# Sooner swaps, a denser opening and a last layer on 128 rows in a convolution and SwiGLU kernel

## The chip, the cores and the metric

The kernel runs on one core of one Trainium2 chip. The metric is the device time of one execution in microseconds (us). Of the kernel before, three timed executions and one profiled execution are shown.

## What is computed

An input `x` of 8 sequences of 4096 tokens with 192 channels goes through a causal depthwise filter of 7 taps (each of 8 heads has its own softmaxed taps for its 24 channels), and the result through a SwiGLU block with 1536 hidden columns.

```python
w = softmax(weight)                       # 8 heads x 7 taps
x_unf = x_pad[:, idx, :]                  # windows of 7 tokens, zeros ahead of the sequence
out = einsum('hk,bskhg->bshg', w, x_unf)  # 24 channels for each head
g, val = x @ w_gate, x @ w_val            # 192 -> 1536, on 32768 tokens
return (silu(g) * val) @ w_out            # 1536 -> 192
```

## The kernel before

**Blocks, chunks, pairs.** The 32768 tokens are 64 blocks of 512. Each block has 12 chunks, one for each 128 hidden columns. Two blocks are a pair, and the filter is made pair by pair: 32 pairs of 24 chunks. The 192 channels are 128 (A) and 64 (B or C).

**First layer.** `Block.first` makes a chunk's gate and value: three steps, and in each step one product on rows 0 to 63 of the array (gate, L428) and one on rows 64 to 127 (value, L429). The two run side by side. Because both halves of the channels must pass through both halves of the array, each filtered tile `xc` has a copy `xs` with its halves swapped. `swapped` (L339) makes it with two transfers from SyncE's queue (L341, L342). `Block.gate` then applies silu on ScalarE (L433) and multiplies with the value on VectorE into `h` (L435). Gates have two banks of PSUM, values three, in rotation.

**Second layer.** `Block.piece` (L440) multiplies 64 rows of `h` with 64 rows of `w_out`. Its two halves run side by side into two banks of `acc`, in two passes: after the first pass the two banks change their halves. Between the passes stands a mark: an empty instruction in SyncE's queue that waits for the last product of the first pass, and for which the first product of the second pass waits (L335). A half of a block (256 tokens) takes 24 units, four at each chunk. A block's units run one block behind its first layer, apart from the first four, which stand at its own last chunk (`lead=4`). Marks therefore come at chunks 1 and 7, and at chunks 4 and 10 a half is complete: ScalarE copies it (L478), SyncE stores it (L470).

**The filter.** Three groups make a pair: g=0 (A of the first block), g=1 (B of both), g=2 (A of the second). Each is transposed on VectorE, its taps are shared out among ScalarE (L365, L358), VectorE (L375) and GpSimd (L380, L387), and GpSimd's last sum writes `xc` (L393). VectorE's running sum starts in a bank of PSUM of its own (`run`). `plan_group` puts each step behind a chunk by `PLAN`. For g=0, 1 and 2, `start` is -16, -24 and -8, and `swap` is counted from there: the swaps stand behind chunks -5, -11 and +7 of the pair, and `load` puts the next pair's loads of x behind chunks 1, 2 and 8 of a block. `opening` has the same steps for pair 1, its last number being the swap.

**Order.** Every engine works off its instructions in the order written. SyncE's queue holds loads, swaps, marks and stores in one order, so that what waits in it holds all that follows.

**Opening and end.** Pair 0 has a filter of its own. Products of zeros into `idle` (`warm`) precede it; `turn_a` transposes x, `spread(0)` multiplies the softmaxed taps out to 128 rows, VectorE makes diagonals (L284) of them, and `conv_a` (L304) filters on TensorE. Its results D0, D1 and D2 are copied by ScalarE (L495 to L499). Behind the last block, `run` makes the rest of its second layer in four banks, in two passes with marks between them, and two stores of 256 tokens follow (L631 to L647).

Of the kernel before, what the change touches and what calls it, by code (L numbers as in the profile page):

```python
# [12 lines left out]
PLAN = dict(  # L13
    start=(-16, -24, -8), turn=-2,
    acts=((3, 5), (2, 4), (2, 4)), dves=(1, 3), pool=4, join=5, npool=(2, 2, 3),
    swap=(11, 13, 15),
    load=((2, -47), (3, -40), (0, -34), (1, -28)),
    opening=(
# [3 lines left out]
    ),  # L22
    gate=2, val=3, lead=4,
)


# [1 line left out]
def kernel(  # L28
# [9 lines left out]
    nc = tc.nc  # L38
    fp32 = mybir.dt.float32
# [9 lines left out]
    P = 128  # L49
    DB = D - P  # L50
    grp = D // H
    SUBS = 4
    TB = P * SUBS
    NCH = Dff // P
# [4 lines left out]
    n_pairs = NT // (2 * TB)  # L59
# [22 lines left out]
    def emit_load(q, part):  # L82
        head = q % ppb == 0
        if part == 2:
            squares[q, "A"] = headA if head else xpool.tile(
                [P, HIST + 2 * TB], fp32, tag="sqA", name="sqA"
            )
            squares[q, "B"] = headB if head else xpool.tile(
                [P, HIST + TB], fp32, tag="sqB", name="sqB"
            )  # L90
        for k in range(2):
            quad = 2 * (part % 2) + k
            if part < 2:
                tile_, t0, n, c = squares[q, "A"], 0, 2 * TB, SQ * quad
            else:
                tile_, t0, n, c = squares[q, "B"], TB * (part % 2), TB, P + SQ * k
            skip = HIST if head and t0 == 0 else 0
            row = q * 2 * TB + t0 - HIST + skip
            n = n // SQ + 1 - skip // SQ
            nc.sync.dma_start(  # L100
                out=tile_[quad * SQ : (quad + 1) * SQ, skip:].rearrange("p (n c) -> p n c", c=SQ),
                in_=x_flat[row : row + n * SQ, c : c + SQ].rearrange("(n p) c -> p n c", p=SQ),
            )
# [19 lines left out]
    for lo, hi in ((0, 2), (2, SUBS), (SUBS, 2 * SUBS)):  # L123
        nc.sync.dma_start(
            out=x_sb[:, lo:hi, :],
            in_=x_flat[lo * P : hi * P, :].rearrange("(s p) d -> p s d", p=P),
# [5 lines left out]
    wo_r = wpool.tile([P, NCH, D], fp16, tag="wo_sb", name="wo_sb")  # L132
# [5 lines left out]
    def load_w(lo, hi, which):  # L138
# [15 lines left out]
        out=mask, in_=mask, pattern=[[1, D]],  # L154
# [3 lines left out]
        out=mask, in_=mask, pattern=[[-1, D]],  # L158
# [33 lines left out]
    for b in range(2):  # L192
# [22 lines left out]
    early = {  # L215
        n: pool0.tile(shape, dt, tag=n, name=n)
        for n, shape, dt in (
            ("xtA", [P, TB], fp32),
            ("xtC", [P, DB + TB], fp16),
            ("sum0", [P, TB], fp32),  # L220
            ("sum1", [P, TB], fp32),
            ("idle", [P, TB], fp32),
            ("sum2", [P, TB], fp32),
# [5 lines left out]
    def warm(*repeats):  # L229
        for r in repeats:  # L230
            nc.tensor.matmul(  # L231
                early["idle"][:, 0 : r * P].rearrange("p (r c) -> p r c", c=P), zeros,
                zeros.unsqueeze(1).to_broadcast([P, r, P]), start=True, stop=True,
            )
# [11 lines left out]
    def turn_a(subs):  # L246
        for s in subs:
            ins = nc.tensor.matmul(  # L248
                early["xtA"][:, ts(s, P)], x16[:, s, colA], ident, start=True, stop=True
            )  # L250
        return ins
# [3 lines left out]
    def spread(g):  # L255
        nc.tensor.matmul(  # L256
            early[f"taps{g}"], (mask[:, 0:P], own)[g], raw, start=True, stop=True
        )

    warm(*6 * (SUBS,))  # L260
    turned = turn_a((0, 1))

    if n_pairs > 1:
        sync_after(nc.sync.nop(), turned, "squares after x")
        for part, _ in PLAN["load"]:
            emit_load(1, part)
    spread(0)
    turn_a((2, 3))
    warm(SUBS, 2)

    xcA, xcC, xcC1, xcA1 = (
        const_pool.tile([P, pad + TB], fp16, tag=n, name=n) for n in ("xcA", "xcC", "xcC1", "xcA1")
# [6 lines left out]
    hi = const_pool.tile([P, 2, K], fp16, tag="hi", name="hi")  # L279
    lo = const_pool.tile([P, K], fp16, tag="lo", name="lo")  # L280
# [20 lines left out]
    def conv_a(d, first):  # L301
        for k in range(K):
            for r, bank in ((slice(0, DB), "sum0"), (slice(DB, P), "sum1")):
                nc.tensor.matmul(  # L304
                    early[bank], d[r, k, :], xcA[r, k : k + TB],
                    start=first and k == 0, stop=not first and k == K - 1,
                )
# [37 lines left out]
    class Group:  # L345
# [24 lines left out]
        def dve_tap(self, k, last):  # L370
            v, s = self.tap(k)
            run = self.aD
            if last:
                self.aD = cpool.tile([P, TB], fp32, tag="aD", name="aD")
            nc.vector.scalar_tensor_tensor(  # L375
                out=self.aD, in0=v, scalar=s, in1=run, op0=ALU.mult, op1=ALU.add
            )
# [21 lines left out]
    class Block:  # L399
# [19 lines left out]

        def first(self, j, steps=range(3)):  # L420
            if 0 in steps:
                self.g[j] = gpool.tile([P, TB], fp32, tag="gate", name="gate")
                self.v[j] = vpool.tile([P, TB], fp32, tag="val", name="val")
            g, v, f = self.g[j], self.v[j], ts(j, P)
            lo, hi = self.operands()
            for i in steps:
                (a, ca), (b, cb) = lo[i], hi[i]
                nc.tensor.matmul(g, w[0:DB, ca, f], a[0:DB, :], start=(i == 0), stop=(i == 2))  # L428
                nc.tensor.matmul(v, w[DB:P, cb, f], b[DB:P, :], start=(i == 0), stop=(i == 2))  # L429
# [52 lines left out]
    D0, D1, D2, D2b = (  # L482
        const_pool.tile([P, TB], fp16, tag=n, name=n) for n in ("D0", "D1", "D2", "D2b")
    )
# [5 lines left out]
    def tapA1(k, xt=None):  # L490
        return (xt or early["xtA1"][:, DB - pad :])[:, k : k + TB], wn[:, 0, k : k + 1]
# [3 lines left out]
    nc.scalar.copy(D0, early["sum0"])  # L495
    nc.scalar.copy(D1, early["sum1"])
    nc.scalar.copy(xcC1, early["xtC1"][:, DB - pad :])
    nc.scalar.mul(actA1[1], *tapA1(5, xcA1))
    nc.scalar.copy(D2, early["sum2"])  # L499
    v, s = tapA1(0)  # L500
    nc.vector.tensor_scalar(sumA1, v, scalar1=s, scalar2=None, op0=ALU.mult)
    for k in range(1, 4):
        v, s = tapA1(k)
        nc.vector.scalar_tensor_tensor(
            out=sumA1, in0=v, scalar=s, in1=sumA1, op0=ALU.mult, op1=ALU.add
# [3 lines left out]
    v, s = tapA1(6, xcA1)  # L509
# [11 lines left out]
    gpool = ctx.enter_context(tc.tile_pool(name="gates", bufs=PLAN["gate"], reuse_waits="tile", space=bass.MemoryType.PSUM))  # L521
    vpool = ctx.enter_context(tc.tile_pool(name="vals", bufs=PLAN["val"], reuse_waits="tile", space=bass.MemoryType.PSUM))
    tpool = ctx.enter_context(tc.tile_pool(name="run", bufs=1, reuse_waits="tile", space=bass.MemoryType.PSUM))
    apool = ctx.enter_context(tc.tile_pool(name="acc", bufs=1, reuse_waits="tile", space=bass.MemoryType.PSUM))
# [66 lines left out]
    lead = PLAN["lead"]  # L591
    before = None
    at = 0
    for n in range(2 * n_pairs):
        block = Block(n)
        for j in range(NCH):
            src, units = before if j < NCH - lead // 4 else block, 4
            if n == 0:
                src, units = block, lead if j == NCH - 1 else 0
            los, his = src.second(units)  # L600
            half = src.done // (2 * NCH) - 1 if units and src.done % (2 * NCH) == 0 else None
            if n == 0 and j < 2:
                if j == 0:
                    block.first(0, (0, 1))
                    block.first(1, (0, 1))
                block.first(j, (2,))
            elif half is None:
                block.first(j)
            for lo, hi in zip(los, his):
                lo()  # L610
                hi()
            if half is not None:
                src.evacuate(half)
                block.first(j)
            block.gate(j)
            if half is not None:
                src.store(half)
            for f in todo.pop(at, ()):
                f()
            at += 1  # L620
        before = block

    acc = before.acc
    other = (
        tpool.tile([P, TB], fp32, tag="run", name="run"),
        vpool.tile([P, TB], fp32, tag="val", name="val"),
# [1 line left out]
    banks = [acc[:, 0, 0:D], acc[:, 1, 0:D], other[0][:, 0:D], other[1][:, 0:D]]  # L628
    before.o = opool.tile([P, SUBS, D], fp32, tag="o", name="o")

    def run(lo, hi, js, first):  # L631
        for j in js:
            before.piece("lo", lo, j, banks[lo], first)
            before.piece("hi", hi, j, banks[hi], first)

    run(0, 1, range(lead, NCH - 2), True)
    run(2, 3, range(NCH - 2), True)
    for j in range(NCH - 2, NCH):
        run(0, 1, (j,), True)
        run(2, 3, (j,), True)  # L640
    run(1, 0, range(NCH), False)
    nc.scalar.copy(before.o[:, 0:2, :], acc[:, :, 0:D])
    before.store(0)
    run(3, 2, range(NCH), False)
    nc.scalar.copy(before.o[:, 2, :], banks[2])
    nc.vector.tensor_copy(before.o[:, 3, :], banks[3])
    before.store(1)  # L647
# [1 line left out]
_INS = ['x', 'weight', 'moe_w_gate', 'moe_w_val', 'moe_w_out']  # L649
_OUTS = [((32768, 192), 'float32')]  # L650
# [25 lines left out]
```

## Time and profile before

| | |
|---|---|
| median of the timed executions | 774.33 us (773.66, 774.33, 775.95) |
| the profiled execution's own time | 775.39 us |
| its span, first to last instruction | 773.7 us |
| TensorE busy | 767.7 us, 99% |
| VectorE, ScalarE, GpSimd busy | 661.3, 664.5, 671.4 us |

PE is TensorE, PEld its weight loads, DVE VectorE, ACT ScalarE, POOL GpSimd, SPq SyncE's queue. A row of the timeline gives start and duration in us, engine, line, operation, output and inputs with their shapes, and how many equal instructions it merges. A bracket gives the idle time ahead of it and what ended that. Rows of TensorE include some 0.2 us of pipeline behind the last product. In the chain of waits a row gives start, duration, and the engine or transfer that the end of the program depended on there.

### The profile page before, as it was taken

The numbers are of one execution on the slowest core, as the hardware profiler recorded it, in microseconds if no ns is written. First come the engines' busy times: TensorE is split into PE (matmuls) and PEld (weight loads), VectorE is DVE, ScalarE is ACT, GpSimd is POOL, SyncE is SP. The second block draws the span as 40 slices with busy tenths as digits, with TensorE's granted clock in tenths as the row PEclk, the third lists the DMA queues.
The fourth block names the chain that finished last, engine by engine and source line by source line (L and its number), as shares of the span: only waits on it lengthen the run. The fifth ranks groups of instructions, "written<-read, shape, count | busy, mean of one in ns | idle before, by whom it ended". The sixth has DMA issues, their size and how long they took to land.

```text
span 773.7 us, 27856 instructions
## 1 busy us (share of the span) xinstructions
PE 767.7 (99%) x10824; PEld 614.8 (79%) x10824; DVE 661.3 (85%) x1045; ACT 664.5 (86%) x1191; POOL 671.4 (87%) x647
## 2 busy tenths in 40 slices
PE   9999999999999999999999999999999999999998
PEld 3788888888777777788878888888777777877787
DVE  7988888888888889888888888888888888888875
ACT  6988888888888888888888888888888888888874
POOL 8899998888988889988889988889888899888850
PEclk9999999999999999999999999999999999999999
DMA  9433434433444343444334344333443433443211
GB/s 180 81 78 79 96 83 96 95 78 81 87 93 89 82 93 78 86 93 96 76 82 94 84 95 87 86 79 84 98 88 81 88 86 85 93 92 81 63 50 53
DMA packets 254900, 67.07 MB, mean 87 GB/s; under 512 B 207792, under 2 KB 254768, under 8 KB 254768
## 3 DMA queue, kind: packets, MB, share of 16 engines
q1 hardware_dynamic: 251952, 63.53, 38.3%
q0 software_dynamic: 2800, 1.77, 1.7%
q8 instruction: 84, 1.38, 0.8%
q14 instruction: 48, 0.39, 0.2%
q10 hardware_dynamic: 16, 0.00, 0.0%
HBM read 29.55 MB, written 25.17 MB: 71 GB/s over the span
## 4 chain that ended last, share of the span: by engine, by line
PE 96%; DMA 2%; ACT 1%; SPq 0%; issue 0%; DVE 0%
PE val L429 44%; PE acc L440 33%; PE gate L428 18%; DMA xs<-xc 2%; PE sum L304 1%; PE idle L231 0%; ACT silu L433 0%; SPq L341 0%; PE val L440 0%; PE sum L311 0%; ACT t L358 0%; PE xtC L242 0%; PE xtA L248 0%; ACT run L365 0%; PE taps L256 0%
## 5 line engine op out<-in xcount | busy, mean ns | idle before, releaser
L435 DVE TENSOR_TENSOR h<-silu,val 128x512 f16<-128x512 f16 x768 | 509.2, 680 | 101.6 <-ACT silu L433 71.9
L433 ACT ACTIVATE silu<-gate 128x512 f16<-128x512 f32 x768 | 453.1, 594 | 80.7 <-PE gate L428 72.0
L440 PE MATMUL acc<-wo_sb,h 64*128 64x192 f16 x6096 | 458.5, 243 | 0.0
L387 POOL TENSOR_TENSOR t<-t,t 128x512 f32<-128x512 f32 x310 | 394.0, 1271 | 62.0 <-ACT t L358 41.7
L440 PEld LDWEIGHTS <-h 64*128 64x128 f16 x6144 | 398.0, 94 | 55.5 <-SPq L335 0.5
L428 PE MATMUL gate<-xc,w_sb 64*128 64x512 f16 x1116 | 409.7, 376 | 0.0
L429 PE MATMUL val<-xc,w_sb 64*128 64x512 f16 x1116 | 409.7, 376 | 0.0
L429 PE MATMUL val<-xs,w_sb 64*128 64x512 f16 x1128 | 364.5, 376 | 1.1 <-DMA xs<-xc 1.0
L428 PE MATMUL gate<-xs,w_sb 64*128 64x512 f16 x1128 | 364.5, 376 | 0.0
L429 PEld LDWEIGHTS <-w_sb 64*128 64x128 f16 x2304 | 208.8, 94 | 78.3 <-issue 2.2
L428 PEld LDWEIGHTS <-w_sb 64*128 64x128 f16 x2304 | 209.1, 94 | 12.6 <-issue 3.5
L393 POOL TENSOR_TENSOR xc<-t,aD 128x512 f16<-128x512 f32 x93 | 118.2, 1270 | 7.3
L380 POOL TENSOR_SCALAR t<-xtA,wn 128x512 f32<-128x512 f32 x155 | 106.2, 696 | 1.5 <-DVE xtA L111 1.5
L358 ACT ACTIVATE t<-xtA,wn 128x512 f32<-128x512 f32 x124 | 88.4, 713 | 0.0
L478 ACT COPY o<-acc 128x384 f32<-128x384 f32 x126 | 60.4, 479 | 16.5 <-PE acc L440 7.3
L375 DVE SCALAR_TENSOR_TENSOR aD<-xtA,wn,run 128x512 f32<-128x512 f32 x62 | 46.0, 741 | 0.0
L358 ACT ACTIVATE t<-xtB,wn 128x512 f32<-128x512 f32 x62 | 44.1, 713 | 0.0
L365 ACT ACTIVATE run<-xtA,wn 128x512 f32<-128x512 f32 x62 | 42.5, 686 | 0.0
L380 POOL TENSOR_SCALAR t<-xtB,wn 128x512 f32<-128x512 f32 x62 | 42.3, 696 | 0.0
L111 DVE STREAM_TRANSPOSE xtA<-sqA 128x544 f32<-128x544 f32 (+1 forms) x48 | 34.6, 721 | 0.0
L375 DVE SCALAR_TENSOR_TENSOR run<-xtB,wn,run 128x512 f32<-128x512 f32 x31 | 23.2, 749 | 0.0
L375 DVE SCALAR_TENSOR_TENSOR run<-xtA,wn,run 128x512 f32<-128x512 f32 x31 | 23.2, 749 | 0.0
(95 smaller groups left out, 174.9 us busy)
## 6 DMA issues: line engine op xcount, KB each, us to landing
out_dram<-o SPq DMA_DIRECT2D x128, 192.0 KB, 2.5
sqA<-in_x_dram SPq DMA_DIRECT2D x96, 132.0 KB, 3.2
xs<-xc SPq DMA_DIRECT2D x186, 64.0 KB, 2.0
sqB<-in_x_dram SPq DMA_DIRECT2D x96, 68.0 KB, 2.4
headA<-in_x_dram SPq DMA_DIRECT2D x28, 128.0 KB, 2.9
headB<-in_x_dram SPq DMA_DIRECT2D x14, 68.0 KB, 2.5
headB<-in_x_dram SPq DMA_DIRECT2D x14, 64.0 KB, 2.0
w_sb<-in_moe_w_gate_dram POOLq DMA_DIRECT2D x3, 192.0 KB, 5.0
```

The lines of the kernel that those rows point to most:

```text
L358: mul(parts[-1], *self.tap(k))
L365: nc.scalar.mul(self.aD, *self.tap(0))
L375: nc.vector.scalar_tensor_tensor(out=self.aD, in0=v, scalar=s, in1=run, op0=ALU.mult, op1=ALU.add)
L380: self.product(k, lambda t, v, s: nc.gpsimd.tensor_scalar(t, v, scalar1=s, scalar2=1.0, op0=ALU.mult, op1=ALU.mult), self.parts)
L387: nc.gpsimd.tensor_tensor(self.parts[0], self.parts[0], t, op=ALU.add)
L393: nc.gpsimd.tensor_tensor(xc, self.parts[0], self.aD, op=ALU.add)
L428: nc.tensor.matmul(g, w[0:DB, ca, f], a[0:DB, :], start=(i == 0), stop=(i == 2))
L429: nc.tensor.matmul(v, w[DB:P, cb, f], b[DB:P, :], start=(i == 0), stop=(i == 2))
L433: nc.scalar.activation(s, self.g.pop(j), AF.Silu)
L435: nc.vector.tensor_tensor(h, s, self.v.pop(j), op=ALU.mult)
L440: ins = nc.tensor.matmul(acc, self.h[j][r, ts(s, P)], wo_r[r, j, :], start=first and j == 0, stop=not first and j == NCH - 1, skip_group_c ...
L478: nc.scalar.copy(self.o[:, 2 * half : 2 * half + 2, :], self.acc[:, :, 0:D])
```

## The change

- `swap`: the steady swaps stand one chunk sooner for g=0, two for g=1 and two for g=2 (chunks -6, -13 and +5). In the opening those of g=0 and g=1 go from 19 to 18 and from 13 to 11.
- In the opening of g=1, ScalarE's second tap goes from chunk 1 to chunk 4, and GpSimd's join from 4 to 5.
- `spread(0)` stands ahead of the first transposes, a product of 128 columns of zeros ahead of it, and the last zero product has 512 columns instead of 256.
- In block 0 the gates of chunks 4, 7 and 10 take the `run` bank, the others the two gate banks as before.
- D2 is copied ahead of the tap product into `actA1[1]`.
- The last block has no units at its own last chunk. Behind it, 48 products on all 128 rows (`whole`) replace the 96 half-row products, with no marks; the first two subtiles are stored together, the other two each by itself.

```diff
-    swap=(11, 13, 15),
+    swap=(10, 11, 13),
...
-        (9, 11, (12, 13), (12, 13), 12, 13, 19),
-        (None, 1, (1, 1), (1, 1), 4, 4, 13),
+        (9, 11, (12, 13), (12, 13), 12, 13, 18),
+        (None, 1, (1, 4), (1, 1), 4, 5, 11),
...
-    gate=2, val=3, lead=4,
+    gate=2, val=3, lead=4, third=(4, 7, 10),
...
-    warm(*6 * (SUBS,))
+    warm(*6 * (SUBS,), 1)
+    spread(0)
     turned = turn_a((0, 1))
...
-    spread(0)
     turn_a((2, 3))
-    warm(SUBS, 2)
+    warm(SUBS, SUBS)
...
-                self.g[j] = gpool.tile([P, TB], fp32, tag="gate", name="gate")
+                pool, tag = (tpool, "run") if self.n == 0 and j in PLAN["third"] else (gpool, "gate")
+                self.g[j] = pool.tile([P, TB], fp32, tag=tag, name="gate")
...
+    nc.scalar.copy(D2, early["sum2"])
     nc.scalar.mul(actA1[1], *tapA1(5, xcA1))
-    nc.scalar.copy(D2, early["sum2"])
...
+            elif n == 2 * n_pairs - 1 and src is block:
+                units = 0
...
+    acc = apool.tile([P, 2, 512], fp32, tag="acc", name="acc")
...
-    run(0, 1, range(lead, NCH - 2), True)
-    run(2, 3, range(NCH - 2), True)
-    for j in range(NCH - 2, NCH):
-        run(0, 1, (j,), True)
-        run(2, 3, (j,), True)
-    run(1, 0, range(NCH), False)
+    def whole(s, js):
+        for j in js:
+            nc.tensor.matmul(
+                banks[s], before.h[j][:, ts(s, P)], wo_r[:, j, :],
+                start=j == 0, stop=j == NCH - 1, skip_group_check=True,
+            )
...
+    whole(0, range(NCH - 2))
+    whole(1, range(NCH - 2))
+    whole(0, range(NCH - 2, NCH))
+    whole(1, range(NCH - 2, NCH))
     nc.scalar.copy(before.o[:, 0:2, :], acc[:, :, 0:D])
     before.store(0)
-    run(3, 2, range(NCH), False)
-    nc.scalar.copy(before.o[:, 2, :], banks[2])
-    nc.vector.tensor_copy(before.o[:, 3, :], banks[3])
-    before.store(1)
+    whole(2, range(NCH))
+    nc.vector.tensor_copy(before.o[:, 2, :], banks[2])
+    store_sub(2)
+    whole(3, range(NCH))
+    nc.scalar.copy(before.o[:, 3, :], banks[3])
+    store_sub(3)
```

More of the change, by code (lines that the diff above doesn't have):

```diff
@@ L621 @@
         before = block
-    acc = before.acc
+    acc = apool.tile([P, 2, 512], fp32, tag="acc", name="acc")
     other = (
@@ L629, with store_sub @@
     before.o = opool.tile([P, SUBS, D], fp32, tag="o", name="o")
-    def run(lo, hi, js, first):
+    def whole(s, js):
         for j in js:
-            before.piece("lo", lo, j, banks[lo], first)
-            before.piece("hi", hi, j, banks[hi], first)
-    run(0, 1, range(lead, NCH - 2), True)
-    run(2, 3, range(NCH - 2), True)
-    for j in range(NCH - 2, NCH):
-        run(0, 1, (j,), True)
-        run(2, 3, (j,), True)
-    run(1, 0, range(NCH), False)
+            nc.tensor.matmul(
+                banks[s], before.h[j][:, ts(s, P)], wo_r[:, j, :],
+                start=j == 0, stop=j == NCH - 1, skip_group_check=True,
+            )
+    def store_sub(s):
+        t0 = before.n * TB + s * P
+        nc.sync.dma_start(out=out[t0 : t0 + P, :], in_=before.o[:, s, :])
+    whole(0, range(NCH - 2))
+    whole(1, range(NCH - 2))
+    whole(0, range(NCH - 2, NCH))
+    whole(1, range(NCH - 2, NCH))
     nc.scalar.copy(before.o[:, 0:2, :], acc[:, :, 0:D])
     before.store(0)
-    run(3, 2, range(NCH), False)
-    nc.scalar.copy(before.o[:, 2, :], banks[2])
-    nc.vector.tensor_copy(before.o[:, 3, :], banks[3])
-    before.store(1)
+    whole(2, range(NCH))
[4 more added lines that the diff above has]
+    store_sub(3)
 _INS = ['x', 'weight', 'moe_w_gate', 'moe_w_val', 'moe_w_out']
```

## Prediction

> **What bounds the kernel.** I read the page first (busy shares, the chain that ended last, the DMA issues), then the chain in order of time, then the timelines of the queues around the places that it names.
>
> ```profile
> PE 767.7 (99%) x10824; PEld 614.8 (79%) x10824; DVE 661.3 (85%) x1045; ACT 664.5 (86%) x1191; POOL 671.4 (87%) x647
> ...
> out_dram<-o SPq DMA_DIRECT2D x128, 192.0 KB, 2.5
> ...
> xs<-xc SPq DMA_DIRECT2D x186, 64.0 KB, 2.0
> ```
>
> TensorE is busy for 99% of the span, so only what TensorE waits for, or what lies ahead of its first and behind its last product, can give time. The chain shows such waits:
>
> ```profile
> 34.31 0.58 PE acc L440 x13
> ...
> 192.66 0.58 PE acc L440 x13
> 197.14 0.47 SPq L341
> 197.66 3.74 DMA xs<-xc
> 201.44 0.37 PE val L429
> 204.84 0.61 PE acc L440 x13
> ...
> 764.04 0.66 PE acc L440 x14
> ```
>
> One such row comes every half block of the steady state. From 34.31 to 192.66 are 27 halves without a disturbance: 158.35 / 27 = 5.865 us each. From 192.66 to 204.84 are two, which should take 11.73 and took 12.18: 0.45 us went where a half-swapped copy (xs) arrived 3.74 us after its issue, against a median of 2.0. Over all of the steady state, 764.04 - 34.31 = 729.73 us for 124 halves of 5.865, or 727.24: **2.5 us are lost in all**, and the chain's rows have the same DMA in front of them. That is the main thing that the change can remove.
>
> **The swaps.** Here are SyncE's queue and GpSimd's joins around that loss.
>
> ```profile
> 182.22 0.40 SPq L470 DMA_DIRECT2D out_dram<-o  x1
> 185.41 0.47 SPq L341 DMA_DIRECT2D xs<-xc  x1
> ...
> 193.95 0.40 SPq L470 DMA_DIRECT2D out_dram<-o  x1
> 197.14 0.47 SPq L341 DMA_DIRECT2D xs<-xc  x1
> ```
>
> ```profile
> 178.68 1.27 POOL L393 TENSOR_TENSOR xc<-t,aD 128x512 f16<-128x512 f32 x1
> ...
> 193.36 1.27 POOL L393 TENSOR_TENSOR xc<-t,aD 128x512 f16<-128x512 f32 x1
> ```
>
> Group 0's xc is ready at 193.36 + 1.27 = 194.63, yet its swap is issued at 197.14: in SyncE's order it stands behind the two marks of chunk 7, which wait for TensorE. The change puts it after chunk 6, ahead of these marks and next behind the store of chunk 4, whose issue ends at 194.35. So it goes out at about 194.7, 2.4 us sooner for one chunk in the plan. Group 2's (185.41; its xc is ready at 179.95) moves from chunk 7 to 5, behind the store at 182.22, to about 182.7: 2.7 us sooner. Group 1's passes ahead of chunk 1's marks in the same way. The second copy of group 0 arrived at 197.66 + 3.74 = 201.40 and cost TensorE 0.45; 2.4 us sooner the same slow copy is 1.9 us early, and one of the usual 2.0 us over 3. What is late next is nothing on this path: the other operands are older. The copies then share the DMA engines with the loads issued at chunk 2 in place of those of chunk 8; 5 us of latency would still be harmless. I take 2.4 of the 2.5 us; the ends are 1.2 (half of it, as the late transfers come irregularly and another execution may have fewer) and 2.5.
>
> **The opening.** TensorE, and then ScalarE's one row that sets the filter's start:
>
> ```profile
> 4.04 0.59 PE L256 MATMUL taps<-raw,mask 8*128 8x7 f32 x2
> 4.57 0.39 PE L248 MATMUL xtA<-ident,x 128*128 128x128 f16 x2
> 4.75 0.85 PE L231 MATMUL idle<-zeros 128*128 128x512 f16 x2
> 5.63 3.17 PE L304 MATMUL sum<-xcA,dghi 64*128 64x512 f16 x14
> ...
> 10.10 1.69 PE L304 MATMUL sum<-xcA,dglo 64*128 64x512 f16 x14
> ```
>
> ```profile
> 5.00 0.59 ACT L298 CAST xcA<-xtA 128x512 f16<-128x512 f32 x1 [0.68 <-PE xtA L248]
> ```
>
> The filter's first pass at 5.63 starts when xcA is copied (5.00 + 0.59), and that copy follows the last transpose. The tap product goes ahead of all four transposes instead of between the pairs. It then starts some 0.2 us sooner, and the diagonals behind it on VectorE too, but the last transpose stays where it was: what stood ahead of it still does. So the tap's move is worth 0 here. The trailing zero product grows from 256 to 512 columns: at the pace of the 5.63 row (3.17 less about 0.2 of pipeline, over 7 pairs of 512 columns, 0.43 each) that is 0.21 us more, ending at about 5.65 where 5.4 was covered by the copy. With a change from 128 to 64 rows (0.1, below) the pass starts at 5.75: **+0.1 us**, ends 0 and +0.2. One zero product of 128 columns before the tap is covered by the wait for the softmax.
>
> Block 0, in which the gates wait for their banks:
>
> ```profile
> 15.08 1.69 PE L311 MATMUL acc<-xcC,dgC 128*128 128x512 f16 x7
> 16.70 0.39 PE L428 MATMUL gate<-D,w_sb 64*128 64x512 f16 x1
> ...
> 18.39 0.37 PE L428 MATMUL gate<-D,w_sb 64*128 64x512 f16 x1 [0.23 <-ACT silu L433]
> ...
> 24.29 0.56 PE L440 MATMUL acc<-wo_sb,h 64*128 64x192 f16 x8
> ```
>
> ```profile
> 17.75 1.08 ACT L433 ACTIVATE silu<-gate 128x512 f16<-128x512 f32 x2
> ```
>
> ```profile
> 18.38 1.28 DVE L435 TENSOR_TENSOR h<-silu,val 128x512 f16<-128x512 f16 x2
> ```
>
> Ten chunks take 24.29 - 16.70 = 7.59 us; at three pairs of 0.2155 each (half of 0.43, the pace of the 10.10 row) they need 6.47. So 1.1 us are waits for silu to free a bank. A third bank takes these away for chunks 4, 7 and 10, but for chunk 4 it is group 1's running sum, read by VectorE until the products resume at 18.38: that chunk starts no sooner than now (18.39). Behind it VectorE is next. Its products come at 0.64 us (1.28 for two) and chunk 11 needs product 8 out of the three value banks: 18.38 + 7 x 0.64 = 22.9, plus 0.65, is 23.5, so 0.8 us is the most. Against it stands the tap of group 1 that moves from chunk 1 to chunk 4 on ScalarE: it now lies between two silus (0.5 us each), which delays silu 5, its product, and the value bank of chunk 8. Following the queues chunk by chunk with these durations I get back nearly all of the gain: **-0.1 us**, ends -0.8 and +0.3. D2 ahead of the product actA1[1] brings its consumer 0.05 forward, within this; it delays GpSimd's sum for block 1, wanted only at 24.6, by under 1 us, well covered. The opening's swaps at 18 and 11 pass SyncE's marks likewise, with nothing late behind them.
>
> **The tail.**
>
> ```profile
> 768.07 1.93 PEld L440 LDWEIGHTS <-h 64*128 64x128 f16 x48 [0.24 <-SPq L335]
> ...
> 770.29 0.32 ACT L645 COPY o<-run 128x192 f32<-128x192 f32 x1 [0.54 <-PE run L440]
> ```
>
> 48 products on 128 rows replace 96 on half the rows; two halves run side by side, so the columns to stream are equal. The marks between the passes, and their 0.24 us, go. One change of row mode comes: from 15.08 seven products of 0.2155 end at 16.59, and the first half-row product starts at 16.70, so 0.1. Net -0.1. The Trainium skill's TensorEngine Tiling, Key Properties, says that changing the tiling mode drains TensorE: a rule against this edit. The row agrees and bounds it at 0.1 us; had each of the 48 products drained, the tail would lose 5 us, but only the first of them changes the mode. The last store halves to 96 KB, which lies between the page's 64 KB at 2.0 and 192 KB at 2.5: 0.1 to 0.4 sooner, of which I take 0.2. Sum **-0.3**, ends -0.6 and +0.2.
>
> **Sum.** -2.4 + 0.1 - 0.1 - 0.3 = -2.7 us. The profiled execution took 775.39 us (span 773.7), so its like would take 772.7. The median of the runs shown is 774.33, and they spread over 2.3 us, as much as the whole stall: a faster execution may hold less of it. From the median I therefore take 2.4: **771.9 us**.
>
> **Rivals.**
>
> *The clock opens sooner.* The first pass ran at 0.43 us a pair, the second at half of that: TensorE got to full pace between 8.8 and 10.1. If denser zero products bring this ahead of the first pass, it falls from 3.17 towards 1.69; the tap's sums and diagonals then bind sooner, and I take 1.1 of the 1.5. Time 770.8. For it: the gap in TensorE's stream ahead of 4.04 closes. Against: the tap product itself hardly streams, and stays in the middle. The Trainium skill's TensorE: Matmul & The Clock Gate, Part 1, says that the clock is half until TensorE has been busy for a free-running window of about 3.4 us; by that rule the result would differ from run to run. The two passes agree with it; what share of the window counts as busy no row here shows.
>
> *The stall is smaller in most runs, or the transfers still come late.* Transfers of over 5.7 us, or an unprofiled run with 1 us of stall, leaves a gain of 1.0: 773.3. For: the spread of the runs. Against: the slow copy shown took 3.74 us, and from 195.2 to the 200.95 at which TensorE wanted it there are now 5.7.
>
> *SyncE holds TensorE's marks.* Slower. Group 0's swap now stands ahead of chunk 7's marks. xc is ready at 194.63, two issues of about 0.55 end at 195.8, and the marks are due shortly before 197.14, with 0.65 us of gate products behind them: 1.9 us of slack. If GpSimd were 2.06 us later in all 31 pairs, each would cost 0.16, 5.0 in all, less 2.4 gained: 776.9. For: GpSimd is 87% busy and each join ends its queue. Against: nothing in the steady state of this change adds work to GpSimd.
>
> **Chances.** Forecast 0.50 (its own range 771.2 to 772.8), sooner clock 0.22, smaller stall 0.20, marks 0.08. A measurement of this kernel tells about 0.3%, 2.3 us, from no change; the border is 772.0. Of the forecast some 0.36 lies below it: faster 0.36 + 0.22 = 0.58; same 0.14 + 0.20 = 0.34; slower 0.08. The range 770.3 to 774.0 leaves out the marks and the ends of the other cases.
>
> **What would show it.** Right: the chain's rows keep 5.865 us from 34 to 764 with under 0.5 us lost, swaps of group 0 issued within 0.3 us of their join and 5 to 6 us ahead of use, no wait of TensorE for xs. The first pass starts at 5.7 and takes 3.2; block 0's ten chunks take 7.4 to 7.6. In the tail no SPq wait, and one gap of 0.1. Wrong: TensorE waiting for SPq at chunk 8; xs waits that remain; a first pass near 1.7 to 2.5 us (the clock); block 0 under 7.0.

## The result and the profile after

| | before | after |
|---|---|---|
| median of the runs on one chip | 774.72 us (773.66 to 775.95, 4 runs) | 770.99 us (770.91 to 771.08, 4 runs) |
| the profiled execution's own time | 775.39 us | 771.08 us |
| its span | 773.7 us | 769.4 us |

The ratio is 0.9951, with a 95% interval of 0.9934 to 0.9968: 3.7 us faster, where 2.4 were forecast. The median lies inside the stated range (770.3 to 774.0) but below the forecast's own (771.2 to 772.8), beside the 770.8 of the first rival. Between the two profiled executions the span fell by 4.3 us. Laid side by side by the first gate product of each block, the two traces give it to five stretches:

| stretch | before | after | difference | predicted |
|---|---|---|---|---|
| start to the first gate (opening) | 13.59 | 11.92 | -1.67 | +0.1 |
| block 0 | 11.03 | 10.81 | -0.22 | -0.1 |
| block 1 | 11.73 | 12.07 | +0.34 | 0 |
| blocks 2 to 62, over 61 times 11.73 | 2.47 | 0.00 | -2.47 | -2.4 |
| last gate to the end | 8.14 | 7.85 | -0.29 | -0.3 |

The page after has TensorE at the same 99%, and in the rows of DMA issues the stores' median fell from the 2.5 us of before:

```profile
PE 764.2 (99%) x10777; PEld 560.9 (73%) x10777; DVE 660.9 (86%) x1045; ACT 662.3 (86%) x1191; POOL 669.8 (87%) x647
...
out_dram<-o SPq DMA_DIRECT2D x127, 192.0 KB, 2.0
...
xs<-xc SPq DMA_DIRECT2D x186, 64.0 KB, 2.0
```

The chain of waits after (start, duration, engine and line). From 32.72 to 759.98 are 727.26 us, which is 124 halves of 5.865 with nothing lost; no row of DMA stands between them any more.

```profile
32.72 0.66 PE acc L441 x16
...
759.98 0.66 PE acc L441 x16
761.93 2.09 PE acc L637 x24
764.02 0.99 PE run L637 x12
765.01 1.00 PE val L637 x12
```

The timeline of GpSimd and SyncE after, ahead of block 16, the place where the kernel before lost 0.45 us. The join ends at 191.81 + 1.27 = 193.08, and group 0's swap is issued at 193.10. Block 16 begins at 199.0 (11.92 + 10.81 + 12.07 + 14 x 11.73), so the copy goes out 5.9 us ahead of its use. In this trace the slowest steady-state copy whose landing was recorded took 3.8 us from issue to landing, and TensorE waited for none.

```profile
191.81 1.27 POOL L393 TENSOR_TENSOR xc<-t,aD 128x512 f16<-128x512 f32 x1
192.27 0.40 SPq L471 DMA_DIRECT2D out_dram<-o  x1
193.10 0.47 SPq L341 DMA_DIRECT2D xs<-xc  x1
193.62 0.59 SPq L342 DMA_DIRECT2D xs<-xc  x1
```

The timeline of TensorE in the opening after. The first pass starts at 5.70, as forecast, but takes 1.69 us and not 3.17: TensorE was at full pace before it. The second zero product shows it too: the two of the row at 4.87 take 0.59 together, the two at 4.75 before (three quarters of the columns) took 0.85.

```profile
3.83 0.59 PE L256 MATMUL taps<-raw,mask 8*128 8x7 f32 x2
4.36 0.68 PE L248 MATMUL xtA<-ident,x 128*128 128x128 f16 x4
4.87 0.59 PE L231 MATMUL idle<-zeros 128*128 128x512 f16 x2
5.70 1.69 PE L304 MATMUL sum<-xcA,dghi 64*128 64x512 f16 x14 [0.24 <-DVE dghi L284]
...
8.43 1.69 PE L304 MATMUL sum<-xcA,dglo 64*128 64x512 f16 x14
```

Block 0 after, on TensorE: two waits of over 0.2 us are left, and they are the two that the prediction named, group 1's running sum (chunk 4) and the late product behind the moved tap (the value bank of chunk 8).

```profile
16.63 0.37 PE L429 MATMUL gate<-D,w_sb 64*128 64x512 f16 x1 [0.21 <-DVE aD L375]
...
19.93 0.37 PE L430 MATMUL val<-D,w_sb 64*128 64x512 f16 x1 [0.27 <-DVE h L436]
```

Block 1 after, timeline of GpSimd, SyncE and the weight loads. The opening's swap of group 0 waits in SyncE's queue for the join (28.79 + 1.27 = 30.06), then takes two issues to 31.34. The mark for which the second pass of the second layer waits is behind it, and the first weight load of that pass stands 0.28 us:

```profile
28.79 1.27 POOL L393 TENSOR_TENSOR xc<-t,aD 128x512 f16<-128x512 f32 x1
...
30.09 0.47 SPq L341 DMA_DIRECT2D xs<-xc  x1
30.61 0.73 SPq L342 DMA_DIRECT2D xs<-xc  x1
...
31.53 0.31 PEld L441 LDWEIGHTS <-h 64*128 64x128 f16 x8 [0.28 <-SPq L335]
```

The tail after, timeline. The 12 products between 763.85 and 764.84 take 0.0825 us each, on all rows. The last gate pair starts at 761.56 and occupies 0.2155, to 761.78, and the first product on 128 rows starts at 761.86: one gap of 0.08. No row has a wait for SyncE.

```profile
761.56 0.38 PE L430 MATMUL val<-xc,w_sb 64*128 64x512 f16 x1
...
761.86 2.15 PE L637 MATMUL acc<-wo_sb,h 128*128 128x192 f16 x24
...
763.85 1.15 PE L637 MATMUL run<-wo_sb,h 128*128 128x192 f16 x12
...
764.84 1.15 PE L637 MATMUL val<-wo_sb,h 128*128 128x192 f16 x12
```

### The profile page after: what moved, and what is told of

The parts are those of the page before. It is cut to its first block, busy times and chain, and to the rows that moved or that the text cites. A ratio compares the mean times of both kernels' runs of the same rounds, so it can differ in the third digit from the quotient of the medians.

```text
span 769.4 us, 27759 instructions
## 1 busy us (share of the span) xinstructions
PE 764.2 (99%) x10777; PEld 560.9 (73%) x10777; DVE 660.9 (86%) x1045; ACT 662.3 (86%) x1191; POOL 669.8 (87%) x647
## 4 chain that ended last, share of the span: by engine, by line
PE 98%; DVE 1%; ACT 0%; issue 0%; DVEq 0%
PE gate L429 52%; PE acc L441 32%; PE val L430 12%; PE sum L304 0%; PE idle L231 0%; PE acc L637 0%; PE sum L311 0%; DVE h L436 0%; ACT silu L434 0%; DVE dghi L284 0%; PE val L637 0%; PE run L637 0%; DVE aD L375 0%; DVE run L375 0%; PE xtC L242 0%
## 5 line engine op out<-in xcount | busy, mean ns | idle before, releaser
L441 PEld LDWEIGHTS <-h 64*128 64x128 f16 x6048 | 312.0, 94 | 106.0 <-SPq L335 0.8
L441 PE MATMUL acc<-wo_sb,h 64*128 64x192 f16 x6048 | 375.3, 243 | 0.0
```

Source lines behind the costliest of these rows:

```text
L441: ins = nc.tensor.matmul(acc, self.h[j][r, ts(s, P)], wo_r[r, j, :], start=first and j == 0, stop=not first and j == NCH - 1, skip_group_c ...
```

## The experiments

Twelve kernels were run, four at a time on one chip, each set beside 35 runs of the kernel before (medians 773.55, 773.42 and 773.96, each from about 771.6 to between 776.5 and 778.2). Besides the times, each left one trace. This table is cut from the traces in the same way as the one above: "full pace" is where the trace's record of the granted clock begins, "excess" is blocks 2 to 62 over 61 times 11.73.

| kernel | full pace at | first pass | first gate | block 0 | block 1 | excess | tail |
|---|---|---|---|---|---|---|---|
| before | 9.40 | 3.17 | 13.59 | 11.03 | 11.73 | 2.47 | 8.14 |
| after | 4.57 | 1.69 | 11.92 | 10.81 | 12.07 | 0.00 | 7.85 |
| s1, swaps alone | 4.95 | 1.69 | 11.87 | 11.03 | 11.73 | 0.11 | 8.06 |
| s2, opening alone | 3.90 | 1.69 | 11.81 | 11.03 | 11.73 | 1.29 | 8.16 |
| s3, tail alone | 5.43 | 1.69 | 11.74 | 11.03 | 11.73 | 0.95 | 7.98 |
| s4, block 0 alone | 9.35 | 3.17 | 13.63 | 10.81 | 11.91 | 0.56 | 8.18 |
| a2, after once more | 6.04 | 1.81 | 12.09 | 10.80 | 12.09 | 0.00 | 7.84 |
| r1, old opening | 13.82 | 3.17 | 15.62 | 10.80 | 12.13 | 0.00 | 7.81 |
| r2, old opening swaps | 6.40 | 1.97 | 12.28 | 10.80 | 11.92 | 0.12 | 7.88 |
| b1, no block 0 edits | 7.05 | 2.31 | 12.59 | 11.03 | 11.73 | 0.10 | 7.89 |
| r3, old zeros | 6.66 | 2.23 | 12.28 | 10.80 | 12.06 | 0.00 | 7.86 |
| r4, old tap place | 4.45 | 1.69 | 11.72 | 10.81 | 11.95 | 0.08 | 7.88 |
| e1, one zero product more | 6.68 | 2.02 | 12.51 | 10.81 | 12.08 | 0.00 | 7.84 |
| q1, swap of group 0 alone | 4.00 | 1.69 | 11.57 | 10.81 | 12.06 | 0.04 | 7.90 |

### Each part alone, on the kernel before

**s1, the swaps.**

```diff
-    swap=(11, 13, 15),
+    swap=(10, 11, 13),
```

> The kernel before with the steady swaps alone sooner (10, 11, 13 instead of 11, 13, 15). Theory: late copies cost 2.5 us in the profile of before and none behind block 1 in the profile after, so this alone gives -1.9 to -2.5 us, and its times spread over less than 1 us because the irregular transfers no longer reach TensorE. Rival (most of the gain is the clock of the opening, and unprofiled runs hold little stall): under -1.2 us, with the spread of before.

Measured: 772.09 us (771.24 to 773.27, 12 runs), ratio 0.9983 (0.9972 to 0.9995). Excess 0.11 for 2.47. But the runs fall into two groups, six at 771.24 to 771.53 and six at 772.64 to 773.27, and the trace, of a run at 771.24, shows the opening at full pace. This kernel's opening is that of before, untouched:

```profile
5.65 1.69 PE L304 MATMUL sum<-xcA,dghi 64*128 64x512 f16 x14 [0.29 <-ACT xcA L298]
...
8.38 1.69 PE L304 MATMUL sum<-xcA,dglo 64*128 64x512 f16 x14
```

So the 1.67 us of the opening are not bound to the changed opening: they come and go from one execution to the next.

**s2, the opening.**

```diff
-    warm(*6 * (SUBS,))
+    warm(*6 * (SUBS,), 1)
+    spread(0)
     turned = turn_a((0, 1))
...
-    spread(0)
     turn_a((2, 3))
-    warm(SUBS, 2)
+    warm(SUBS, SUBS)
```

> The kernel before with the opening alone changed: the tap product ahead of the first transposes, one more product of 128 columns of zeros, the last zero product with 512 columns. Theory: the clock comes ahead of the first filter pass, whose 14 products take 1.7 us instead of 3.2; the first gate starts 1.6 to 1.8 us sooner, and the time falls by 1.2 to 1.8 us. Rival (the clock comes by chance, whatever the zeros): the pass takes 3.2 us here as before, and the time moves by +0.1 us.

Measured: 772.15 us (771.47 to 774.77, 12 runs), ratio 0.9985 (0.9969 to 1.0000). First pass 1.69. With the swaps of before, the stall is there, but half as long as in the trace of before: 1.29 us. The chain of waits of s2, at its longest:

```profile
571.61 0.47 SPq L341
572.13 3.66 DMA xs<-xc
575.84 0.37 PE val L429
```

**s3, the tail.** The edit is the last two parts of the change's diff (no units at the last block's own last chunk, and `whole`).

> The kernel before with the last block's second layer on 128 rows, its stores and the missing units of its last chunk alone. Theory: from the last gate product to the end of the span -0.3 us (7.84 instead of 8.14), one gap of 0.1 us where the rows change, no wait for SyncE's marks. Rival (each product on 128 rows loads its weights in the open, some 0.05 us each): +2 us.

Measured: 772.63 us (771.30 to 775.05, 12 runs), ratio 0.9991 (0.9978 to 1.0005), not to be told from no change. In the trace the tail takes 7.98 us; in the traces with the old tail it takes 8.06 to 8.18, in the others with the new one 7.81 to 7.90. The mean of the four old ones is 8.14 and of the ten new ones 7.87: -0.26.

**s4, block 0.** Third bank, the tap at chunk 4 and the join at 5 for group 1, D2 first; the opening's swaps stay where they were.

> The kernel before with block 0 alone changed: the third gate bank for chunks 4, 7 and 10, the tap of group 1 at chunk 4 and its join at 5, D2 ahead of the tap product. Theory: from the first gate of block 0 to that of block 1 -0.2 us (10.8 instead of 11.03), as chunk 4 still waits for the running sum and chunk 8 for a value bank. Rival (the third bank takes the waits for silu away): -0.8 us.

Measured: 773.37 us (771.54 to 775.79, 12 runs), ratio 0.9995 (0.9980 to 1.0011): no change. Block 0 takes 0.22 less and block 1 gives 0.18 back. Timelines of VectorE and TensorE at chunk 6 of block 1, first of s4, then of before:

```profile
29.99 0.65 DVE L436 TENSOR_TENSOR h<-silu,val 128x512 f16<-128x512 f16 x1
```

```profile
30.30 0.38 PE L429 MATMUL gate<-xA,w_sb 64*128 64x512 f16 x1
30.34 0.32 PE L441 MATMUL acc<-wo_sb,h 64*128 64x192 f16 x2
30.69 0.37 PE L430 MATMUL val<-xA,w_sb 64*128 64x512 f16 x1
```

```profile
29.96 0.65 DVE L435 TENSOR_TENSOR h<-silu,val 128x512 f16<-128x512 f16 x1
```

```profile
30.49 0.38 PE L428 MATMUL gate<-xA,w_sb 64*128 64x512 f16 x1
30.66 0.37 PE L429 MATMUL val<-xA,w_sb 64*128 64x512 f16 x1
```

The gate of chunk 6 starts 0.19 us sooner (30.30 for 30.49), its value product at the same time (30.69, 30.66). In both kernels that value starts as VectorE's product ends (29.99 + 0.65 = 30.64; 29.96 + 0.65 = 30.61), and these products did not come sooner. The bank freed TensorE; VectorE's chain of products was the bound behind it.

### What the opening is worth

The two groups of s1 made a test possible: on kernels whose steady state loses nothing, a run in which full pace comes late stands out by 1.5 us or more. No run of these kernels lies between 772.15 and 772.54, so I call one over 772.4 late. That a late run is one with a late clock is seen in one trace only (r1's, below); for the others it is inferred from their times.

**a2, the changed kernel once more** (no edit).

> The changed kernel once more, for the spread of its runs. The kernel with the swaps alone fell into two groups, 771.24 to 771.53 and 772.64 to 773.27 us, and its profiled execution (of the first group) had TensorE at full pace before the first filter pass, which took 1.69 us as in the changed kernel and not 3.17 as before. Theory A (the changed opening brings the full clock forward for good): all runs lie in one group, 770.8 to 771.2. Theory B (the moment of the full clock is drawn anew in each execution, whatever the opening, and the profiled ones of before and after happened to differ): about half of the runs lie 1.4 to 1.7 us higher, near 772.4 to 772.7.

Measured: 771.20 us (770.70 to 773.43, 11 runs), ratio 0.9967 (0.9950 to 0.9985). Two of 11 are late (772.88, 773.43). Neither theory holds as it stood: late runs do occur, but not in half of the executions.

**r1, the changed kernel with the opening of before** (the diff of s2 reversed).

> The changed kernel with the opening of the kernel before (zero products and tap product as they were). Theory A: two groups, about half of the runs at 770.9 to 771.2 and half at 772.3 to 772.9; median above that of the changed kernel run beside it, by up to 1.5 us. Theory B: the same two groups, in the same shares as the changed kernel run beside it; medians alike.

Measured: 772.71 us (770.87 to 774.80, 12 runs), ratio 0.9980 (0.9963 to 0.9997). Seven of 12 are late. The means of r1 and a2, 772.38 and 771.47, are 0.9 apart, from 12 and 11 runs that spread over 3.9 and 2.7 us. The trace of r1 is of a very late one, with both filter passes at half pace, 2 x 1.48 us more than in the trace of after:

```profile
5.76 3.17 PE L304 MATMUL sum<-xcA,dghi 64*128 64x512 f16 x14
...
10.62 3.17 PE L304 MATMUL sum<-xcA,dglo 64*128 64x512 f16 x14
```

**r3 and r4, one half of the opening's edit each.** r3 has the zero products of before with the tap product still first; r4 has the longer zeros with the tap product back between the pairs of transposes.

```diff
 r3:
-    warm(*6 * (SUBS,), 1)
+    warm(*6 * (SUBS,))
...
-    warm(SUBS, SUBS)
+    warm(SUBS, 2)
 r4:
-    spread(0)
     turned = turn_a((0, 1))
...
+    spread(0)
     turn_a((2, 3))
```

> The changed kernel with the zero products of before (six of 512 columns, and 512 and 256 at the end), the tap product still ahead of all four transposes. Theory: the 384 columns of zeros are what makes windows that end between 5.9 and 7.05 us count; without them about half of the runs are late, as with the whole opening of before (7 of 12), median 772 or above; a profile whose window ends there shows a first pass of 3.17. Rival: the tap product's place does it, and 2 to 4 of 12 are late.

> The changed kernel with the tap product back between the pairs of transposes; the longer zeros stay. Theory: as the changed kernel, 2 to 4 of 12 late, median 770.9 to 771.3. Rival: the tap's place does it, and half are late, median 772 or above.

Measured: r3 771.16 us (770.63 to 772.89, 11 runs), ratio 0.9971 (0.9958 to 0.9983), two late of 11. r4 771.21 us (770.86 to 774.90, 12 runs), ratio 0.9974 (0.9959 to 0.9990), four late of 12. My theory that the zeros alone do it fell with r3, where half of the runs should have been late. Its trace has full pace at 6.66, inside the first pass:

```profile
5.53 2.23 PE L304 MATMUL sum<-xcA,dghi 64*128 64x512 f16 x14
```

Which of the two halves does more, these counts cannot tell.

**e1, one zero product more**, in the 0.2 us in which TensorE waits for the second half of x.

```diff
     turned = turn_a((0, 1))
...
+    warm(2)
     turn_a((2, 3))
```

> The changed kernel with one more zero product of 256 columns between the two pairs of first transposes, where TensorE waits some 0.2 us for the second half of the cast x. Theory: the full clock comes at the end of the first 3.41 us window in which TensorE streamed enough; the changed opening made windows that end between 5.9 and 7.05 us into the span count, which did not count before, and this one adds to the streaming in the same windows. So late executions (1.5 us or more over the lower group) become rarer still: 0 or 1 of 12 runs for 2 of 11 of the changed kernel, median 770.9 to 771.1. Where the clock is still half, the added product costs at most 0.05. Rival: the windows that still fail are those that lie at the other end, with the 1.05 us before TensorE's first product in them; nothing changes, 2 to 4 late runs of 12. Second rival: the product delays the last transpose by its 0.2 us and with it the filter's start: 771.2 in the lower group.

Measured: 771.15 us (770.80 to 771.81, 11 runs), ratio 0.9971 (0.9958 to 0.9983). No run is late, as the theory had it, but the count does not show that the product does it: q1, without the product, has no late run of 11 either. The second rival is right too: where the clock is still half, the products behind the new one are pushed on, and the first pass starts at 5.97, not 5.75. The timeline of e1:

```profile
4.55 0.42 PE L231 MATMUL idle<-zeros 128*128 128x256 f16 x1
4.76 0.42 PE L248 MATMUL xtA<-ident,x 128*128 128x128 f16 x2
4.97 1.06 PE L231 MATMUL idle<-zeros 128*128 128x512 f16 x2
5.97 2.02 PE L305 MATMUL sum<-xcA,dghi 64*128 64x512 f16 x14
```

**What the counts say together.** With the opening of before: 6 of 12 (s1) and 7 of 12 (r1), 13 of 24. With the whole changed opening: after 0 of 4, a2 2 of 11, r2 3 of 11, b1 4 of 12 and q1 0 of 11, together 9 of 49; such a difference comes by chance about 3 times in 1000 (Fisher's exact test). The sets come from different chips; on the one chip that ran r1 it is 7 of 12 against 9 of 34, about 8 times in 100. With one half of it, 6 of 23, which is not told apart from either.

The traces show what happens. The stretch at full pace lasted 761.172, 764.585 or 767.999 us in all fourteen: 223, 224 or 225 times 3.4133 us. So the clock changes only on a grid of 3.4133 us. Full pace came at 3.90, 4.00, 4.45, 4.57, 4.95 and 5.43 in traces of either opening, and at 6.04, 6.40, 6.66, 6.68 and 7.05 in those of a changed one, half or whole. With the old one the grid points at 5.99 (before, 9.40 less 3.41), 5.94 (s4) and 6.99 (r1) were passed over, and the next ones or the one after came at 9.40, 9.35 and 13.82.

The Trainium skill's TensorE: Matmul & The Clock Gate, Part 1, says that full pace comes after a busy window of 3413 ns that is free-running and does not begin with the kernel. The grid in the traces agrees with it. What the runs add is that the draw also depends on the work ahead of the first pass. How, an estimate says, from the starts of the products in the traces (columns at half pace, the small tap products counted as nothing): the three windows of the old opening that were passed over hold 2.3 to 2.4 us of streaming out of 3.41, the five of a changed opening that counted hold 2.5 to 2.6. So the density in the window is the likely cause. It is not shown as a threshold, since windows that ended at 3.58 (r1) and 3.64 (b1) hold 2.5 and 2.6 by the same estimate and were passed over.

### Block 0, its price in block 1, and the swaps apart

**r2, the opening's swaps back.**

```diff
-        (9, 11, (12, 13), (12, 13), 12, 13, 18),
-        (None, 1, (1, 4), (1, 1), 4, 5, 11),
+        (9, 11, (12, 13), (12, 13), 12, 13, 19),
+        (None, 1, (1, 4), (1, 1), 4, 5, 13),
```

> The changed kernel with the opening's swaps of groups 0 and 1 back at the places of before (19 and 13 for 18 and 11); the swaps of the steady state stay. Theory: the 0.16 us at chunk 8 of block 1, where TensorE waits for a mark behind the swap of group 0 in SyncE's queue, goes; the 0.19 us at chunk 6, where the value product waits for VectorE, stays, as VectorE's chain of products through blocks 0 and 1 sets it. Block 1 then takes 11.9 us for 12.07, and the runs are 0.1 to 0.2 us below those of the changed kernel. Rival: both waits come from SyncE's queue, and block 1 falls to 11.73, runs 0.3 lower.

Measured: 771.35 us (771.00 to 774.95, 11 runs), ratio 0.9973 (0.9957 to 0.9989). Block 1 falls to 11.92: the 0.16 at chunk 8 is gone, the 0.19 at chunk 6 stays, as the theory said. In the seven traces with the new opening swaps that wait costs 0.04 (r4) to 0.21 (r1). The time does not show the gain: the median is not below a2's, and the trace loses 0.12 us at chunk 8 of block 26. There s1 and b1 lose 0.08 and 0.09, but so does r4 (0.08), which has the new opening swaps. At that place a weight load waits for SyncE's mark some 1.8 us behind the last swap's issue, so no join holds the mark; what does is open.

**b1, no edits in block 0.** The changed kernel with `third`, the tap, D2, the join and the opening's swaps as before.

> The changed kernel without any of its edits to block 0 (third gate bank, the tap of group 1, the order of D2, the opening's swaps and join); steady swaps, opening and tail stay. Theory: block 0 takes 11.03 for 10.81 and block 1 11.73 for 12.07, in all 0.1 us less than the changed kernel: 770.8 to 770.9 where that is at 771.0. Rival: the block 0 edits are worth 0.1 or more to the whole, and this kernel is at 771.1 to 771.3.

Measured: 771.38 us (770.73 to 773.25, 12 runs), ratio 0.9975 (0.9959 to 0.9991). Blocks 0 and 1 take 11.03 + 11.73 = 22.76, for 22.88 in after and 22.89 in a2. From the first gate to the end b1 takes 757.46 us, a2 757.44, r2 757.43 and after 757.45: the five edits to block 0 and its swaps are worth nothing, either way.

**q1, group 0's swap alone.**

```diff
-    swap=(10, 11, 13),
+    swap=(10, 13, 15),
```

> The changed kernel with the steady swaps of groups 1 and 2 as before (13 and 15); only group 0's is sooner (10 for 11). Theory: eight of the nine stalls of the kernel before stand at chunk 0 of a block, where group 0's copies are wanted, so this swap alone takes away 2.3 of the 2.5 us: steady stretch 715.5 to 715.8 us, runs as the changed kernel's. Rival: the nearness of the three swaps and of the loads on the DMA engines made the copies slow, and moving one alone leaves half of the stalls: steady stretch over 716.5, runs 1 us higher.

Measured: 771.41 us (770.79 to 772.15, 11 runs), ratio 0.9970 (0.9956 to 0.9983). Excess 0.04: in this trace the one swap that is wanted at the start of a pair does it all. The chain of waits of q1, 759.68 - 32.36 = 727.32 us for 727.26 of undisturbed halves:

```profile
32.36 0.66 PE acc L441 x16
...
759.68 0.66 PE acc L441 x16
```

The theory read the places of the stalls too simply. Of the eight at chunk 0 in before, three stand in the second block of a pair (blocks 45, 55 and 61, 0.32 us in all), where group 2's copies are wanted and not group 0's. SyncE and TensorE of before at block 45: the first copy landed at 542.12, and the product on it starts at 542.16.

```profile
538.33 0.47 SPq L341 DMA_DIRECT2D xs<-xc  x1
...
542.16 0.37 PE L428 MATMUL gate<-xs,w_sb 64*128 64x512 f16 x1
```

The four traces with the old swaps lose 5.27 us together: 4.07 at group 0's places, 0.65 at group 2's (none in s4), and 0.12 each at chunk 2 of block 34, where a weight load waits for SyncE's mark. One trace of q1 without a stall at group 2's places does not show that its swap may stay. The runs hint that it may not: their mean is 771.47, while e1's is 771.18, and those of r3 and r4 without their late runs 771.06 and 771.07, on the same chip.

No version among the twelve can be told from the changed kernel as faster. e1 has the narrowest spread (770.80 to 771.81), but the same median as a2.

## Why the prediction was right, and where its steps were wrong

**The swaps: the mechanism was right, the size right for the one trace and too large for the kernel.** The step named the join, SyncE's queue and the copies, with 2.4 of 2.5 us; 2.47 went between the two traces. Group 0 is the main cause: 2.03 of the 2.47 stand at its places, and moving its swap alone leaves 0.04 in q1. But the profiled execution of before held the longest stall of those traced. Four traces have the old swaps, and their excess is 2.47, 1.29, 0.95 and 0.56: 1.3 us in the mean. s1's median lies 1.5 below that of before. The prediction's second rival, "the stall is smaller in most runs", described the kernel better than the forecast did, although the step against it ("the slow copy ... there are now 5.7") was right also: copies still take up to 3.8 us in after, and TensorE no longer waits for them. One premise was wrong. "The late transfers come irregularly" holds for how late they are, not for where: in before, stalls stand at blocks 16, 32 and 48, 26 and 58, 45 and 61, each 16 or 32 blocks apart. In after, all 26 steady-state copies with a recorded time of over 2.8 us went out in blocks 7, 8, 9, 13 and 15 and in those 16, 32 and 48 further on. What comes round every 16 blocks is open.

**The opening: this step failed.** It had +0.1, with a first pass that "takes 3.2". The geometry was right: with the clock still half at its start, a2's and b1's first passes start at 5.75, just as worked out (for 5.63 before). The step put the clock's start at nothing ("the tap's move is worth 0 here"); it was missing from the sum, though the first rival named it, and it is the 1.67 us between the two traces. The rival was wrong on one point too. It made the change the cause of the single difference; s1 and s3 show the same 1.69 with the old opening. What the changed opening moves is the share of late runs, from 13 of 24 to 9 of 49. A late run costs 1.5 us in s1 (means of its two groups) and 2.5 in r1, so this is worth about 0.36 x 1.5 to 2.5, or 0.5 to 0.9 us on average. That is an estimate, and it rests on the pooled counts; r1 against a2 measured 0.9.

**Block 0: sign and places right, one sentence wrong.** -0.1 was forecast, -0.22 came, with the two waits that the step named. "The opening's swaps ... pass SyncE's marks likewise, with nothing late behind them" was wrong: the swap of group 0 waited for its join in SyncE's queue, a mark was late, and r2 takes this wait away. It was the third rival's mechanism, in the one pair where GpSimd's join is late enough, and it cost 0.16 in after. The step also ended at block 0's last chunk, while VectorE carried the rest of the gain away in block 1 (s4).

**The tail: the sum right, its parts not.** -0.3 forecast, -0.29 between the traces, -0.26 over all of them; one gap of 0.08 where 0.1 was taken, and no wait for SyncE. But 0.2 of it was put on the last store, and the store gave nothing. The one 96 KB store whose landing the trace after records took 1.6 us, against a median of 2.0 for 192 KB. Yet from the last store's issue to the end of the span it is 2.99 us in both traces, 770.69 to 773.68 and 766.38 to 769.37:

```profile
770.69 0.37 SPq L470 DMA_DIRECT2D out_dram<-o  x1
...
766.38 0.35 SPq L644 DMA_DIRECT2D out_dram<-o  x1
```

The first row is of before, the second of after. The 0.29 lie ahead of these issues: 0.21 from the last gate to the end of TensorE's last product (4.69 and 4.48 us), and 0.09 from there to the issue (0.47 and 0.38). So the products and marks were worth twice the 0.1 taken. Why the end does not follow the sooner landing, no run here tests.

**The sum.** -2.7 for the profiled execution was short of -4.3 by the clock (-1.67 for +0.1), of which blocks 0 and 1 took 0.2 back (+0.12 together for -0.1). For the median the two errors of size were opposite: about -1.3 for the swaps where -2.4 was taken (0.3 of it given back for the spread), and about -0.7 for the opening where +0.1 was. With +0.1 for blocks 0 and 1 and -0.3 for the tail, -1.3 - 0.7 + 0.1 - 0.3 is -2.2; the means of a2 and of before on the same chip, 771.47 and 773.64, are 2.2 apart. The range held, and the number came close partly by luck, because two mis-sized terms made up for each other. The 3.7 us of the first comparison had the luck of four early runs of four.

## What to carry to other kernels

A single trace of a kernel with rare stalls and a clock that starts at its own moment is one draw: before a stall's length is put into a forecast, compare it with the spread of the plain run times (here 2.3 us in three runs, 4.8 to 6.5 in 35), and count how many executions hold it. A transfer that waits behind marks in one queue is best issued as soon as its data are ready, and the one whose user comes first carries most of the gain (here 4.07 of 5.27 us in the four traces with the old swaps). A bank or a slot given to the engine that waits moves the wait to the next engine in the chain; follow that chain to the end of the next stage before counting the gain.

## What the runs showed of the hardware

- TensorE's stretch at full pace lasted 223 to 225 times 3.4133 us in all fourteen traces, so it starts on a grid of that step. The start was drawn anew in each execution: 3.90 to 13.82 us into the span, and block 0 began 3.7 us later in r1 than in after (15.62 and 11.92), with the same block 0 behind it.
- With the old opening, grid points at 5.94, 5.99 and 6.99 us were passed over; with the tap product first (r3), or with that and longer zeros, points at 6.04 to 7.05 counted. Denser streaming in the window is the likely cause, by the estimate above. No trace shows what the longer zeros do alone: r4's full pace came at 4.45.
- The clock column of the windows view does not show the slow start. In before, this row of it has a granted clock of 1.00 (the column behind POOL), while the first pass in it ran at 0.43 us a pair. In the opening the pace has to be read from the products, or from where the record of the clock begins.

```profile
5.00:7.00 2.00, 1.97 (x10) 0.71 (x10) 1.93 (x5) 1.97 (x3) 1.11 (x3) 1.00 1.07 162
```

- Copies of 64 KB from SyncE, all of the same shape, took 1.9 us in the median (L341) and up to 3.8 in the steady state of after (4.0 in before). The slow ones come back every 16 blocks, 188 us. The longest time of after, 5.5 us, is that of the first such copy of all (xs<-xA), issued at 16.0 us.
